# Softmax turned without normalising: inverted sums through DRAM scale the product with v, and both full tiles of even head pairs go by the crossbar (56 for 28)

## The chip, the cores and the metric

The kernel runs on one core of a Trainium2 chip. The metric is the device time of one execution in microseconds. Three executions of the kernel before took 923.4, 923.61 and 923.7 us; the median is 923.61. The engines are TensorE (PE, with its weight loads PEld), VectorE (DVE), ScalarE (ACT), GpSimd (POOL) and SyncE (SP), which here only issues DMAs.

## The reference

Attention over 8 batches of 8 heads (576 tokens, 64 features each). Scores more than tau below their row's maximum drop out before the softmax. A feed-forward part follows: a first product, relu, a convolution of three taps over the tokens, a gate, and a second product.

```python
scores = scale * np.matmul(q, k.transpose(0, 1, 3, 2))
thresh = np.max(scores, axis=-1, keepdims=True) - tau
scores = np.where(scores >= thresh, scores, -1000000000.0)
scores = scores - np.max(scores, axis=-1, keepdims=True)
attn = np.exp(scores)
attn = attn / (np.sum(attn, axis=-1, keepdims=True) + 1e-09)
attn_out = np.matmul(attn, v)
...
h = np.maximum(x @ w_in, 0.0)
conv_out += conv_w[k][None, None, :] * hp[:, k:k + S, :]
gate = 1.0 / (1.0 + np.exp(-conv_out))
return (h * gate @ w_out)
```

## The kernel before

The tokens of a batch are cut into tiles of 128 (four full ones and a last one of 64), and these into two chunks: tiles 0 and 1, and tiles 2, 3 and 4. The heads of a batch form four pairs; one pair of one chunk is a *pair* in what follows (64 in all, numbered 0 to 63), and one tile of one pair is a *unit* (160 in all). Odd pairs run their tiles backwards. Batch 0 ("plain") takes a path in full float32 and also prepares the weights; batches 1 to 7 split their operands into a high and a low part.

For each unit, `unit` (line 563) has TensorE compute the scores of both heads into PSUM (`ps_s`), VectorE take the negated maximum of a row (L599), ScalarE the exponential into `em` (L608), and VectorE the mask, which also adds up the rows into `few` (L611). Then come a guard against sums of zero (L628), the reciprocal (L635), an even share for a row whose sum is zero (L632), and the normalising of `em` in place, 128 x 576 for each head (L644, on POOL but for a few).

The normalised weights must be turned so that keys lie on partitions. `transposes` (L685) lets TensorE do it: for a full tile two groups of four 128 x 128 blocks and one block of a third group, which the tiles of a pair share (L703); ScalarE copies them out of PSUM (`ps_t`, two buffers) into `eT` (L698). For one full tile of each even pair of batches 1 to 7, 28 units in all, `cross` (L659) does it by DMA: ScalarE and POOL split `em` into low and high 16-bit halves (`parts`, L326 and L328), a DMA writes them to DRAM (`rows`, L676), and two DMA transposes read them back through the crossbar into `eT` (L681). `CROSS = (1, 0)` says how many full tiles of an even and an odd pair go that way.

`attend` (L746) multiplies `eT` with v into `pa`, which takes the same PSUM buffers as the transposes. From the third chunk on, two pairs are done together (28 joint products). ScalarE copies the result as the high part of `x` (L774), and VectorE subtracts for the low part (L777). `mm1` and `mm2` are the feed-forward products (`ph` and `po`), which run interleaved with the attention of the next chunk.

The order on each engine is fixed when the program is built: `Plan` simulates the engines with a planned duration for each step (the number after the engine's name in `op`), takes what is ready with the smallest rank minus `ahead`, and emits the instructions in that order. A step with `other` may go to another engine when its own has a backlog. DMAs are steps too (`put`, or `op("sp", ...)` with a `ring` cost). Each engine, SP included, works off its instructions in order and waits where its next one isn't ready. A buffer is free for its next use when its last reader is done; `eT`, `v`, `ps_t` have two each, `em` five.

## Time and profile before

| | before |
|---|---|
| median of three executions | 923.61 us |
| the profiled execution | 925.83 us, its span 924.0 us |
| mean granted TensorE clock | 0.989 |
| transposes on TensorE (L703) | 1060 |
| DMA transposes (L681) | 56 |
| normalising on POOL (L644) | 285, 258.5 us busy |

The page of a profile gives busy time, share of the span and number of instructions for each engine, then the chain of work that ended last, and the costliest groups of instructions: `line engine operation out<-in shapes xcount | busy us, mean ns of one | idle us of the engine just before them <- what ended most of it`. Rows of the view by windows give the length of a stretch, for each engine its busy us and (x number of instructions), then the granted clock, the share of the 16 DMA engines that is busy, and GB/s. Rows of waits read `engine line waited for: us in total, times, longest us`. A row of the chain or the timeline begins with its start and its length in us. TensorE's matmuls overlap one another, so the length of one is more than what it adds to the queue.

### The profile page before, as it was taken

To read this page: it belongs to the slowest core of one execution; us is meant where nothing else is said; L and a number is where in the kernel's file an instruction comes from. 1 tells how busy PE (TensorE), PEld (TensorE's weight loads), DVE (VectorE), ACT (ScalarE), POOL (GpSimd) and SP (SyncE) were. 2 spreads that over 40 slices of the span, in tenths; PEclk is the share of its full clock that TensorE was granted. 3 is DMA by queue.
4 is the path that set the end of the run, shared out by engine and by line. 5 is a ranking of instruction groups with operands and counts; after the bars stand their busy time and mean duration, and the time that the engine had idled before them with its cause. 6 is when DMAs were issued, how large, how long until landed. Compare 5 with 4: busy or idle time off the path is not lost.

```text
span 924.0 us, 18493 instructions
## 1 busy us (share of the span) xinstructions
PE 883.6 (96%) x6056; PEld 709.9 (77%) x6056; DVE 775.4 (84%) x1863; ACT 684.6 (74%) x1450; POOL 636.5 (69%) x1044
## 2 busy tenths in 40 slices
PE   5879899999999999999899999999999999999998
PEld 2445578768879788878778788887868878887897
DVE  5989999988998789987789779996979879998543
ACT  5868688778877787878668687877857778786643
POOL 3656867877777677876667778886866858785422
PEclk9989999999999999999899999999999999999999
DMA  5545137546563565526645275536647076543000
GB/s 207 168 152 158 44 113 210 120 132 181 141 172 76 153 178 158 148 73 175 166 123 126 86 183 138 158 92 181 169 114 180 29 194 169 131 120 100 14 23 35
DMA packets 120927, 122.28 MB, mean 132 GB/s; under 512 B 72320, under 2 KB 88960, under 8 KB 120832
## 3 DMA queue, kind: packets, MB, share of 16 engines
q1 hardware_dynamic: 119968, 119.20, 47.7%
q10 hardware_dynamic: 864, 1.90, 0.6%
q8 instruction: 49, 0.80, 0.4%
q14 instruction: 46, 0.38, 0.1%
HBM read 66.22 MB, written 25.95 MB: 100 GB/s over the span
## 4 chain that ended last, share of the span: by engine, by line
PE 63%; DVE 12%; ACT 10%; POOL 6%; DMA 5%; issue 4%; SPq 1%; ACTq 0%; DVEq 0%; POOLq 0%
PE po L853 17%; PE ph L795 13%; PE pa L767 10%; PE ps_s L591 9%; PE ps_t L703 9%; DVE em L611 4%; ACT em L608 3%; PE ps_s L584 3%; DVE few L599 3%; DMA xq<-in_qd_dram 2%; ACT eT L698 2%; POOL em L644 2%; PE pa L758 2%; DVE t L817 2%; DVE t L822 2%
## 5 line engine op out<-in xcount | busy, mean ns | idle before, releaser
L644 POOL TENSOR_SCALAR em<-em,few 128x576 f32<-128x576 f32 x285 | 258.5, 915 | 34.0 <-DVE few L635 22.4
L611 DVE SCALAR_TENSOR_TENSOR em<-ps_s,few,em 128x576 f32<-128x576 f32 x288 | 230.6, 812 | 38.2 <-ACT em L608 25.4
L608 ACT ACTIVATE em<-ps_s,few 128x576 f32<-128x576 f32 x288 | 210.4, 741 | 51.7 <-DVE few L599 43.1
L599 DVE TENSOR_REDUCE few<-ps_s 128x1 f32<-128x576 f32 x288 | 212.3, 749 | 35.5 <-PE ps_s L591 17.3
L795 PE MATMUL ph<-x,w1h 128*128 128x322 f32 (+1 forms) x1024 | 240.0, 306 | 0.9 <-ACT hp L810 0.6
L698 ACT ACTIVATE eT<-ps_t 128x512 f32<-128x512 f32 (+2 forms) x360 | 168.2, 487 | 31.2 <-PE ps_t L703 28.3
L795 PEld LDWEIGHTS ph<-x,w1h 128*128 128x128 f32 x1024 | 175.6, 191 | 6.3 <-issue 3.2
L703 PE MATMUL ps_t<-ident,em 128*128 128x128 f32 x1060 | 160.3, 280 | 9.6 <-POOL em L644 5.0
L591 PE MATMUL ps_s<-ks,q 128*128 128x288 f32 x896 | 158.9, 307 | 8.5 <-DVE em L611 5.9
L703 PEld LDWEIGHTS ps_t<-ident,em 128*128 128x128 f32 x1060 | 126.2, 143 | 34.4 <-POOL em L644 14.6
L795 PE MATMUL ph<-x,w1l 128*128 128x322 f32 (+1 forms) x512 | 151.9, 297 | 0.0
L591 PEld LDWEIGHTS ps_s<-ks,q 128*128 128x128 f32 x896 | 129.9, 190 | 26.7 <-issue 7.4
L333 POOL TENSOR_TENSOR gl<-t,gh 128x255 fp32r<-128x255 f32 (+9 forms) x192 | 122.7, 652 | 27.9 <-ACT gh L832 26.5
L767 PE MATMUL pa<-eT,v 128*64 128x320 f32 (+1 forms) x1024 | 132.1, 409 | 0.0
L853 PE MATMUL po<-w2h,gh 128*128 128x512 f32 x288 | 119.0, 413 | 0.4 <-ACT hp L810 0.4
L767 PEld LDWEIGHTS pa<-eT,v 128*64 128x64 f32 x1024 | 70.3, 137 | 59.4 <-issue 15.9
L853 PE MATMUL po<-w2h,gl 128*128 128x512 f32 x288 | 113.6, 395 | 0.2
L853 PE MATMUL po<-w2l,gh 128*128 128x512 f32 x288 | 113.5, 394 | 0.0
L817 DVE SCALAR_TENSOR_TENSOR t<-hp,cr 128x321 f32<-128x321 f32 (+1 forms) x128 | 85.1, 668 | 20.2 <-ACT hp L810 20.1
L795 PEld LDWEIGHTS ph<-x,w1l 128*128 128x128 f32 x512 | 97.7, 191 | 0.3
L817 DVE SCALAR_TENSOR_TENSOR t<-hp,cr,t 128x321 f32<-128x321 f32 (+1 forms) x128 | 91.9, 719 | 0.4
L824 ACT ACTIVATE t<-t,cm 128x321 f32<-128x321 f32 (+1 forms) x128 | 68.3, 534 | 28.3 <-DVE t L817 17.6
(81 smaller groups left out, 1147.9 us busy)
## 6 DMA issues: line engine op xcount, KB each, us to landing
v<-in_vc_dram SPq DMA_DIRECT2D x64, 288.0 KB, 3.9
rows<-parts SPq DMA_DIRECT2D x28, 576.0 KB, 3.2
k<-in_kp_dram SPq DMA_DIRECT2D x35, 320.0 KB, 3.5
out_dram<-ot SPq DMA_DIRECT2D x36, 256.0 KB, 2.1
xq<-in_qd_dram SPq DMA_DIRECT2D x28, 320.0 KB, 3.7
xk<-in_kt_dram SPq DMA_DIRECT2D x28, 288.0 KB, 3.3
ks<-xk SPq DMA_DIRECT2D x56, 144.0 KB, 3.6
xq<-in_qd_dram SPq DMA_DIRECT2D x28, 256.0 KB, 3.7
```

Source lines behind the costliest of these rows:

```text
L333: engines[e].tensor_tensor(dst, x, y, op=ALU.subtract)
L591: nc.tensor.matmul(ps[:, c, :CH], lhsT=q[:, h, o:o + n], rhs=k[:, h, c * CH:(c + 1) * CH], start=(i == 0), stop=(i == 1))
L599: nc.vector.tensor_reduce(few[:rows, nm], ps[:rows, :, :CH], op=ALU.max, axis=mybir.AxisListType.XY, negate=True)
L608: nc.scalar.activation(view(), ps[:rows, :, :CH], AF.Exp, bias=few[:rows, nm])
L611: nc.vector.scalar_tensor_tensor(view(), ps[:rows, :, :CH], few[:rows, th], view(), op0=ALU.is_ge, op1=ALU.mult, accum_out=few[:rows, total])
L644: engines[e].tensor_scalar(sl, sl, by, to, op0=ALU.mult, op1=ALU.add)
L698: "act", act(w, True), lambda dst=dst, src=src: nc.scalar.activation(dst(), src(pt), AF.Copy),
L703: nc.tensor.transpose(out=pt[:, at:at + P], in_=em[:, int(b * P):int(b * P) + P], identity=ident[:])
L767: nc.tensor.matmul(pa[j * D:(j + 1) * D, :w], lhsT=vt[:, blk, :], rhs=eT[:, :w // D, blk, :], start=False, stop=(r == 3))
L795: nc.tensor.matmul(ph[:, :an], lhsT=w1[w][:, cb, fs], rhs=xs[cb][:, h, :an], start=(cb == 0 and i == 0), stop=(cb == NCB - 1 and i == 2))
L817: nc.vector.scalar_tensor_tensor(t[:, :kn], hp[:, k:kn + k], cr[:, j, f:f + 1], y, op0=ALU.mult, op1=ALU.add)
L853: nc.tensor.matmul(po[:], lhsT=x[:, f, at:at + P], rhs=w[:, f, :], start=(f == 0 and i == 0), stop=(f == NFB - 1 and i == 2))
```

## The change

`em` is no longer normalised. The masked sums go into one tile `tot` per pair (a column for each tile and head), and when all units of the pair are masked, `invert` guards and inverts them, stores them as a row in DRAM (an element of four bytes per partition and tile, one or two DMAs per head) and loads that row back, spread over the 64 partitions of each head (`inv`). The product with v is then multiplied by `inv` on VectorE (`xn`), and the high and low part of `x` are taken from `xn`, the low part on POOL. A row whose sum is zero gets its even share from a tiny constant instead: ScalarE adds 2^-80 while it copies transposes out of PSUM, and the high halves of crossed tiles are raised to the bits of that value (a maximum on POOL). `CROSS = (2, 0)` sends both full tiles of an even pair by DMA, 56 units instead of 28. `em` has four buffers instead of five.

```diff
-NORM = (('pool',), ('pool',))
-NEAR = 8
+EVEN = 2.0 ** -80
+EVEN_TOP = 0x1780
+INVS = 2
+PARTS = 2
-EMS = 5
-CROSS = (1, 0)
+EMS = 4
+CROSS = (2, 0)
...
             def mask(ps=ps, th=th, view=view, total=total):
                 nc.vector.scalar_tensor_tensor(
                     view(), ps[:rows, :, :CH], few[:rows, th], view(), op0=ALU.is_ge, op1=ALU.mult,
-                    accum_out=few[:rows, total]
+                    accum_out=tot[:rows, total]
                 )
...
-        op("dve", 112, guard, w=[(few, "inverse")], r=ss, ahead=a, port=True, other=tiny)
-        op("dve", 82, lambda: nc.vector.reciprocal(few[:rows, inverse], few[:rows, inverse]), w=[(few, "inverse")], ahead=a)
-        op("dve", 124, even, w=[(few, "shift")], r=ss, ahead=a, port=True, other=tiny)
-        for h in range(m):
-            def norm(e, h=h):
...
+    def invert(i, p, n, tot):
+        cols, a = 2 * (n // P) + (n % P > 0), AHEAD["a"]
+        spread = plan.buf(wk, "inv", INVS, [P, S - QW], F32, f"inv_{i}")
+        row = plan.buf(far, "row", INVS, [2, S - QW], F32, f"row_{i}")
+        ts = [(tot, j) for j in range(cols)]
         def guard(e):
+            engines[e].tensor_scalar(tot[:, :cols], tot[:, :cols], S * EVEN, 1.0, op0=ALU.add, op1=ALU.mult)
+        op("dve", 112, guard, w=ts, ahead=a, port=True, other=[("pool", 200)])
+        op("dve", 82, lambda: nc.vector.reciprocal(tot[:, :cols], tot[:, :cols]), w=ts, ahead=a)
+        for h in range(2):
+            def out(h=h):
+                nc.sync.dma_start(
+                    row[h, :n // P * P].rearrange("(t q) -> q t", q=P), tot[:, :n // P * 2].rearrange("q (t h) -> q t h", h=2)[:, :, h]
+                )
+            op("sp", 500, out, w=[(row, h)], r=ts, ahead=a, ring=n // P * P * 1.6)
+            if n % P:
+                op(
+                    "sp", 500, lambda h=h: nc.sync.dma_start(row[h, n // P * P:n].rearrange("(q e) -> q e", e=1), tot[h * D:(h + 1) * D, cols - 1:cols]),
+                    w=[(row, 2 + h)], r=ts, ahead=a, ring=D * 1.6
+                )
+        for h in range(2):
+            j = h ^ p % 2
+            put(
+                n, lambda h=h, j=j: nc.sync.dma_start(spread[j * D:(j + 1) * D, :n], row[h:h + 1, :n].broadcast_to([D, n])),
+                issue=500, rows=D, w=[(spread, j)], r=[(row, h)] + ([(row, 2 + h)] if n % P else []), ahead=a
+            )
+        return spread
...
-                copy(e, parts[:, j], src)
+                if j:
+                    engines[e].tensor_scalar(parts[:, j], src, EVEN_TOP, None, op0=ALU.max)
+                else:
+                    copy(e, parts[:, j], src)
...
-                    "act", act(w, True), lambda dst=dst, src=src: nc.scalar.activation(dst(), src(pt), AF.Copy),
+                    "act", act(w, True), lambda dst=dst, src=src: nc.scalar.activation(dst(), src(pt), AF.Copy, bias=EVEN),
...
-            def high(pa=pa, x=x, off=off):
-                nc.scalar.activation(x[:, 0, off:off + w], pa[:, :w], AF.Copy)
-            def low(pa=pa, x=x, off=off):
-                nc.vector.tensor_tensor(x[:, 1, off:off + w], pa[:, :w], x[:, 0, off:off + w].bitcast(F32), op=ALU.subtract)
-            op("act", act(w, True), high, w=[(x, 0)], r=[(pa, 0)], ahead=a)
-            op("dve", dve(w), low, w=[(x, 1)], r=[(pa, 0), (x, 0)], ahead=a)
+            xn = plan.buf(wk, "xn", 2, [P, S - QW], F32, f"xn_{i}")
+            def scale(pa=pa, xn=xn, inv=inv):
+                nc.vector.tensor_tensor(xn[:, :w], pa[:, :w], inv[:, :w], op=ALU.mult)
+            def high(xn=xn, x=x, off=off):
+                nc.scalar.activation(x[:, 0, off:off + w], xn[:, :w], AF.Copy)
+            def low(e, xn=xn, x=x, off=off):
+                subtract(e, x[:, 1, off:off + w], xn[:, :w], x[:, 0, off:off + w].bitcast(F32))
+            op("dve", dve(w), scale, w=[(xn, 0)], r=[(pa, 0), (inv, 0), (inv, 1)], ahead=a)
+            op("act", act(w), high, w=[(x, 0)], r=[(xn, 0)], ahead=a)
+            op("pool", pool(w), low, w=[(x, 1)], r=[(xn, 0), (x, 0)], ahead=a, other=[("dve", dve(w))], port=True)
```

The change moves instructions everywhere, since every order is planned anew. Three places matter later. The first is TensorE after the scores of pair 9's first tile (`ps_s`), early in batch 1. Before, it turns the second full tile of pair 8 (`em_1398`) there; in between stands a group of `po` and the scores of the next tile:

```order
L703 MATMUL ps_t_0_1507<-ident,em_1398 128x128 x4
L703 MATMUL ps_t_4_1517<-ident,em_1398 128x128 x4
L853 MATMUL po_1325<-w2h,gh 128x512
L853 MATMUL po_1325<-w2h,gl 128x512
L853 MATMUL po_1325<-w2l,gh 128x512
L591 MATMUL ps_s_0_1534<-ks_1_1357,q_9_1372 128x288
L591 MATMUL ps_s_0_1534<-ks_1_1357,q_9_1448 128x288
L591 MATMUL ps_s_0_1534<-ks_1_1357,q_9_1372 128x288
L591 MATMUL ps_s_0_1534<-ks_1_1357,q_9_1448 128x288
L703 MATMUL ps_t_8_1541<-ident,em_1398 128x128
```

Of the change, the same place (after the product `pa_1464` of pair 7) up to the first transposes, which are of pair 9:

```order
L867 MATMUL po_1309<-w2h,gh 128x512
L867 MATMUL po_1309<-w2h,gl 128x512
L867 MATMUL po_1309<-w2l,gh 128x512
L593 MATMUL ps_s_0_1509<-ks_1_1363,q_9_1408 128x288
L593 MATMUL ps_s_0_1509<-ks_1_1363,q_9_1427 128x288
...
L593 MATMUL ps_s_1_1515<-ks_1_1363,q_9_1408 128x288
L593 MATMUL ps_s_1_1515<-ks_1_1363,q_9_1427 128x288
L711 MATMUL ps_t_0_1526<-ident,em_1481 128x128 x4
```

The nine transposes of pair 8's second tile are gone; what is left on TensorE is the same work in another order.

The second place is SP's queue around pair 20 (a second chunk of batch 2). Before, one half tile (`rows`) goes out, and its two turns stand between the loads of `v`:

```order
L676 DMA rows_3367<-parts_3336 128x2304
L551 DMA k_3372<-in_kp_dram 128x640
L541 DMA xq_3383<-in_qd_dram 128x2x320
L560 DMA v_3428<-in_vc_dram 128x576
L681 DMA_TRANSPOSE eT_3433<-rows_3367 128x9x128 x2
L560 DMA v_3481<-in_vc_dram 128x576
L551 DMA k_3492<-in_kp_dram 128x640
```

Of the change, from that load of `v` on, where `row` is the stored inverse and `inv` its spread:

```order
L561 DMA v_3464<-in_vc_dram 128x576
L689 DMA_TRANSPOSE eT_3473<-rows_3309 128x9x128 x2
L561 DMA v_3530<-in_vc_dram 128x576
L642 DMA row_3537<-tot_3235 128x2x1
L689 DMA_TRANSPOSE eT_3473<-rows_3369 128x9x128 x2
L649 DMA row_3537<-tot_3235 64x1
...
L649 DMA row_3682<-tot_3387 64x1
L684 DMA rows_3721<-parts_3695 128x2304
L655 DMA inv_3729<-row_3537 64x320 x2
L875 DMA out_dram<-ot_3707 128x512
L655 DMA inv_3748<-row_3682 64x320 x2
L684 DMA rows_3770<-parts_3761 128x2304
```

The same stretch of the queue has four turns instead of two, eight stores of inverses and four spreads; half tiles, outputs and the loads of the next pairs stand behind spreads that wait for their stores.

The third place is VectorE, from the reciprocal of pair 21 (`tot_3387`) to the scaling of the joint product of pairs 20 and 21 (`xn_3827`, `xn_3848`). Before, two subtractions that read only the product and its high part stood there:

```order
L635 RECIPROCAL few_3857<-few_3857 128x1
L777 TENSOR_TENSOR x_3676<-pa_3849,x_3676 128x320
L777 TENSOR_TENSOR x_3683<-pa_3852,x_3683 128x320
L599 TENSOR_REDUCE few_3927<-ps_s_0_3910 128x1
L599 TENSOR_REDUCE few_3927<-ps_s_1_3921 128x1
```

Of the change (left out are three more maxima, three limits and three masks):

```order
L639 RECIPROCAL tot_3387<-tot_3387 128x5
L613 SCALAR_TENSOR_TENSOR em_3643,tot_3665<-ps_s_1_3616,few_3636,em_3643 128x576
L601 TENSOR_REDUCE few_3698<-ps_s_0_3684 128x1
...
L613 SCALAR_TENSOR_TENSOR em_3807,tot_3817<-ps_s_0_3782,few_3798,em_3807 128x576
L639 RECIPROCAL tot_3665<-tot_3665 128x5
L784 TENSOR_TENSOR xn_3827<-pa_3790,inv_3729 128x320
L784 TENSOR_TENSOR xn_3848<-pa_3793,inv_3748 128x320
L601 TENSOR_REDUCE few_3860<-ps_s_0_3841 128x1
L601 TENSOR_REDUCE few_3860<-ps_s_1_3854 128x1
```

The scaling stands where the subtraction stood, but reads `inv` too, which comes by two DMAs after the reciprocal at the head of these rows; the maxima of the next scores stand behind it.

40 lines of the change are left out of this document (13 added, 27 removed).

## The prediction

> **What bounds the kernel now.** The views, in order: the page's busy table, the busy times by stretch, TensorE's waits from 120 to 880 us.
>
> ```profile
> span 924.0 us, 18493 instructions
> PE 883.6 (96%) x6056; PEld 709.9 (77%) x6056; DVE 775.4 (84%) x1863; ACT 684.6 (74%) x1450; POOL 636.5 (69%) x1044
> ```
> ```profile
> core 0: us, PE busy (x) PEld busy (x) DVE busy (x) ACT busy (x) POOL busy (x), PEclk, DMA share, GB/s
> 120.00:860.00 740.00, 726.83 (x5128) 601.26 (x5125) 646.98 (x1565) 569.63 (x1207) 549.29 (x897) 0.99 0.53 140
> 0.00:120.00 120.00, 96.33 (x561) 56.17 (x561) 102.04 (x250) 86.07 (x173) 69.38 (x110) 0.96 0.44 141
> 860.00:924.00 64.00, 60.48 (x373) 52.46 (x371) 26.34 (x50) 28.93 (x72) 17.82 (x39) 1.00 0.07 25
> ```
> The average hides three stages. From 120 to 860 us TensorE is idle for only 740.0 - 726.8 = 13.2 us, while VectorE has 93 us to spare: there TensorE's own work sets the pace, and its largest wait there is small:
>
> ```profile
> PE ps_s L591 <- DVE em L611: 5.9, 8, 2.1
> ```
> In the first 120 us TensorE idles 23.7 us and VectorE is the fullest engine (102 of 120, and it also prepares the weights). After 860 us TensorE works off the last products. So work taken off TensorE shortens the middle one for one; work taken off VectorE counts in the first stage; work taken off POOL counts by itself nowhere.
>
> **What leaves TensorE.** In each of 28 even pairs of batches 1 to 7 the second full tile is turned by DMA too. That removes two groups of four transposes and one of the odd ones, nine a tile: 28 x 9 = 252 of 1060 at the line that turns. Their price is read from the chain of waits in a stretch where TensorE never stops, since a matmul's own length overlaps the next one's:
>
> ```profile
> 408.15 0.33 PE ps_t L703 x3
> ...
> 419.70 0.87 PE ps_t L703 x8
> ```
> 0.33/3 and 0.87/8 both give 0.109 to 0.110 us, so 252 x 0.109 = **27.5 us**. No other matmul is added or removed. All of it lies in the stage where TensorE is the bound.
>
> **What leaves the other engines**, by the page's and the grouped rows:
>
> ```profile
> L644 POOL TENSOR_SCALAR em<-em,few 128x576 f32<-128x576 f32 x285 | 258.5, 915 | 34.0 <-DVE few L635 22.4
> ```
> ```profile
> L635 DVE RECIPROCAL few<-few 128x2 f32<-128x2 f32 x128 | 20.3, 159 | 0.7
> L628 DVE TENSOR_SCALAR few<-few 128x2 f32<-128x2 f32 x56 | 20.3, 362 | 1.0
> ```
> The normalising goes (258.5 us of POOL), and the guard, the reciprocal and the even share are no longer done per tile (160 times): one guard and one reciprocal per pair remain (64 each). In the first stage, where VectorE counts, the guard (L628), the even share (L632) and the reciprocal (L635) take on VectorE, in that order:
>
> ```profile
> 0.00:120.00 120.00, 2.02 (x6) 4.05 (x13) 0.96 0.44 141
> 0.00:120.00 120.00, 3.81 (x17) 0.45 (x2) 0.96 0.44 141
> 0.00:120.00 120.00, 2.94 (x19) 0.96 0.44 141
> ```
> 2.02 + 3.81 + 2.94 = 8.8 us. Eight pairs' reciprocals (8 x 0.159) and, of their guards, the share that stays on VectorE (27 of 64 in the new order, so 3.4 x 0.362) put back 2.5. Of the 6.3 us I count the share that VectorE is busy there (85%): **5.3 us**. Bounds: 0, if PE's idle time there comes from loads, and the 23.7 us of that idle time.
>
> **What is added on engines**, by groups of like form:
>
> ```profile
> L698 ACT ACTIVATE eT<-ps_t 128x512 f32<-128x512 f32 x232 | 135.2, 598 | 29.6 <-PE ps_t L703 27.8 <-DMA rows<-parts 0.5
> L326 ACT ACTIVATE parts<-em 128x1152 uint16<-128x1152 uint16 x28 | 32.6, 1166 | 1.8 <-POOL em L644 1.6
> L328 POOL COPY parts<-em 128x1152 uint16<-128x1152 uint16 x27 | 32.8, 1216 | 0.6
> L380 POOL TENSOR_SCALAR stage_f<-stage_f 128x512 f32<-128x512 f32 x16 | 10.3, 648 | 8.3 <-ACT stage_f L377 7.9
> L333 POOL TENSOR_TENSOR gl<-t,gh 128x320 fp32r<-128x320 f32 x8 | 6.9, 868 | 0.3 <-ACT gh L832 0.3
> L777 DVE TENSOR_TENSOR x<-pa,x 128x320 fp32r<-128x320 f32 x32 | 15.6, 486 | 17.0 <-ACT x L774 16.9
> ```
> ACT: 28 more halves (28 x 1.166 = 32.6 us) against 56 evictions of 512 fewer (56 x 0.598 = 33.5): nothing. VectorE: the scaling by the inverse reads PSUM and SBUF as the old subtraction did, 64 at its price, so they cancel. POOL takes that subtraction (64 x at most 0.868 = 56 us) and 56 high halves, now with a maximum. This form is not in the trace: per element between the copy (1216/1152 = 1.06 ns) and the normalising (915/576 = 1.59), so 1.22 to 1.83 us; by the two-limit row (648/512 = 1.27 ns) I take 1.46, 82 us. POOL gains 56 + 82 - 33 = 105 and loses 258: it gets emptier and hides both. Without that cover they would still not count, as TensorE is the bound.
>
> **What is added on DMA and its queue.** 28 more half tiles go out, 56 more turns come in, and new are 192 tiny stores (one element of four bytes per partition and tile) and 128 spreads over 64 partitions. First the page's row of the queue, then SP's timeline, then the windows around it:
>
> ```profile
> q1 hardware_dynamic: 119968, 119.20, 47.7%
> ```
> ```profile
> 475.06 3.18 SPq L681 DMA_TRANSPOSE eT<-rows  x2
> ```
> ```profile
> 476.00:482.00 6.00, 6.00 (x39) 5.22 (x36) 3.79 (x9) 4.12 (x8) 3.21 (x5) 1.00 0.96 228
> ```
> In these 6 us two turns, a load of v and one output keep the engines 0.96 busy. If all of it were the turns', one would cost all 16 engines 2.9 us; with the two plain transfers (288 and 256 KB on the page) taken out by bytes against the 228 GB/s of the row, 1.7. I take 2: 56 x 2 = 112 us, and 114 for half tiles and spreads (an estimate: 28 x 576 KB and 128 x some 72 KB at the same rate). What the tiny stores cost is bounded by the small packets of the turns:
>
> ```profile
> DMA packets 3048, 2.27 MB, mean 189 GB/s; under 512 B 2441, under 2 KB 2441, under 8 KB 3047
> ```
> The row is DMA's for 470 to 482 us: two turns are the only small packets there, 2441 in about 4 us, or 1.6 ns each. The stores write 32 x 2 x (256 + 320) = 36,864 elements: 59 us. So DMA goes from 0.48 x 924 = 444 us to about 729, or 0.81 of the new span: not the bound, but crowded. SP itself issues the 56 turns in 1.6 us each (3.18/2) and some 350 short ones in 0.5 us each (the median of the row below), 265 us more; it has room, since it waits 210 us for outputs alone:
>
> ```profile
> L510 SPq DMA_DIRECT2D ks<-xk x56: 461/538/1156, 94.6 to 777.3; - x56
> ```
> ```profile
> SPq L861 <- ACT ot L860: 210.2, 27, 24.3
> ```
> But the spreads wait on SP for their stores, and behind them stand the loads of the next pairs, the half tiles and the outputs. The Trainium skill, "DMA: Bandwidth & Descriptors", § Rules for kernel authors, speaks against these stores: a last dimension that isn't contiguous becomes one descriptor per element. No row here shows such a store; by the 10.5 ns a packet that the page's § Bandwidth gives for 64 packets, as an estimate, they would take 387 us and fill the engines beyond the span, and the crowding case below would be the likeliest, 909 us.
>
> What does crowding cost TensorE? The trace has two cases (ScalarE's waits of 2.72 and 3.11 us for xq at L553), in which a load came late beside two turns; ACT waited for it, VectorE for ACT, TensorE for VectorE. This is the dearer one, in the timeline and in the windows:
>
> ```profile
> 448.83 0.31 ACT L553 ACTIVATE q<-xq 128x128 f32<-128x128 f32 x1 [2.72 <-DMA xq<-in_qd_dram]
> ...
> 450.75 1.04 PE L591 MATMUL ps_s<-ks,q 128*128 128x288 f32 x4 [1.87 <-DVE em L611]
> ...
> 673.81 0.31 ACT L553 ACTIVATE q<-xq 128x128 f32<-128x128 f32 x1 [3.11 <-DMA xq<-in_qd_dram]
> ```
> ```profile
> 448.00:458.00 10.00, 7.54 (x38) 6.98 (x37) 7.05 (x17) 5.70 (x14) 6.90 (x10) 0.66 0.62 147
> ```
> In these 10 us TensorE idles 10 - 7.5 = 2.5 us, and the granted clock is 0.66 on average, which costs 0.34 x 10 = 3.4 us: 5.9 us for one such stall. I take **one more of them, 5.9 us**; bounds are none, and one at the start of each of seven batches, 41 us. The Trainium skill, "TensorE: Matmul & The Clock Gate", § Part 1: The HAM clock gate, lets the clock halve only after an idle window of about 3.4 us. By that rule a stall of 2.5 us costs no clock, and the sum would be 3.4 us less; the trace disagrees, its clock fell after gaps shorter than that.
>
> The turned tiles themselves should arrive in time (timeline of SP and of TensorE, and the turns' landing):
>
> ```profile
> 416.31 3.51 SPq L681 DMA_TRANSPOSE eT<-rows  x2
> ```
> ```profile
> 438.55 0.77 PE L758 MATMUL pa<-eT,v 64*64 64x320 f32 x8
> ```
> ```profile
> DMA to landing us min/median/max: 3.7/4.6/6.4
> ```
> Four turns instead of two issue in 7 us from 416.3 and land by 428 to 430, some 9 us ahead of the product at 438.55 that reads them.
>
> **The sum**, on the profiled span: 924.0 - 27.5 - 5.3 + 5.9 = 897.1. That execution took 925.8 with what lies around its span, 2.2 over the median of 923.61; I carry the difference of -26.9 over to the median: **896.7 us**.
>
> **The rivals.**
> - *Crowded DMA* (more late loads like the one above): three stalls instead of one give 924.0 - 32.8 + 17.7 - 0.4 = 909 us. For it speaks the share of 0.96 over six us, to which two more turns come; against it, only two such stalls beside 28 crossed tiles now.
> - *The scaling waits for its inverse; this ends slower.* Stores and loads of ks stand in for the two hops (first the output's row, then the one of ks):
>
> ```profile
> DMA to landing us min/median/max: 2.0/2.1/5.0
> ```
> ```profile
> DMA to landing us min/median/max: 2.2/3.5/5.6
> ```
> After the odd pair's reciprocal SP issues four stores (0.5 us each), waits for them, spreads twice (1.0) and lands: 2 + 2.1 + 1 + 3.5 = 8.6 us at the medians, 13.6 at the worst. Between that reciprocal and the scaling VectorE has, in the order shown for the change, five masks, four maxima and the even pair's scaling:
>
> ```profile
> L611 DVE SCALAR_TENSOR_TENSOR em<-ps_s,few,em 128x576 f32<-128x576 f32 x288 | 230.6, 812 | 38.2 <-ACT em L608 25.4
> L599 DVE TENSOR_REDUCE few<-ps_s 128x1 f32<-128x576 f32 x288 | 212.3, 749 | 35.5 <-PE ps_s L591 17.3
> ```
> 5 x 0.812 + 4 x 0.749 + 0.486 = 7.5 us, 8.6 at 87% busy. So the inverse is just in time at the medians and 5 us late at the worst. Behind a waiting scaling stand VectorE's next maxima, and both PSUM buffers of the transposes stay taken, so TensorE runs dry soon after. At the midpoint, 2.5 us late at each of 28 joint products, 70 us: 924.0 - 32.8 + 70 - 0.4 = 961. It turns slower from 32.8/28 = 1.2 us a product. Against it: the worst landings are rare, the even pair's inverse has a whole pair more, and TensorE has FFN products that need neither buffer.
> - *Better than forecast*: an emptier POOL and a shorter way from mask to transposes remove TensorE's 13.2 us too, and no stall is added: 924.0 - 32.8 - 10 - 0.4 = 881.
> - *It doesn't pay*: TensorE's time comes off, but ACT or DMA paces the middle at today's rate: 918 to 923.
>
> **How the numbers follow.** Forecast (884 to 905) 0.70, crowded 0.13, inverse late 0.07, better 0.08, no gain 0.02. The range takes the forecast's own and half of the crowded case, and its upper end some of the inverse's: 884 to 914 us. A measurement tells 0.2% (1.8 us) from no change. Faster: 0.70 + 0.08 + 0.12 = 0.90; within 0.2%: 0.03; slower: 0.07.
>
> **What would show it.** In the new profile: 808 transposes at about 0.109 us in the chain, TensorE busy near 856 us and still above 93% of the span; POOL near 480; no wait of the scaling for a DMA beyond a few us in all; the granted clock at 0.5 in no more than one or two stretches after 120 us; TensorE's idle time in the first 120 us down by some 5 us. Waits of VectorE's scaling for the inverse, of TensorE's products for the turned tiles, or of SP's loads behind the spreads would make the forecast wrong.

## The result, and the profile after

| | before | after |
|---|---|---|
| median of the runs | 923.65 us (4 runs) | 1347.86 us (4 runs) |
| ratio | | 1.458, 95% interval 1.447 to 1.470 |
| profiled span | 924.0 us | 1349.3 us |
| mean granted TensorE clock | 0.989 | 0.858 |

The forecast was 896.7 us, in a range of 884 to 914; the change makes the kernel 46% slower. The page of the changed kernel first: its span, its busy table and its DMA queue (packets, MB, share of 16 engines).

```profile
span 1349.3 us, 18039 instructions
PE 968.8 (72%) x5804; PEld 753.4 (56%) x5804; DVE 767.6 (57%) x1594; ACT 684.6 (51%) x1376; POOL 551.6 (41%) x783
q1 hardware_dynamic: 240480, 161.84, 70.9%
```

No engine is full any more: TensorE had 96% of its span, now 72%. So it waits, and the views of waits say for what. SP's queue, then the engines:

```profile
SPq L655 <- DMA row<-tot: 279.1, 64, 9.4
SPq L875 <- ACT ot L874: 50.3, 7, 20.7
SPq L689 <- DMA rows<-parts: 28.4, 12, 7.0
```
```profile
DVE xn L784 <- DMA inv<-row: 211.1, 34, 16.7
ACT q L543 <- DMA xq<-in_qd_dram: 122.3, 21, 13.1
PE ps_s L593 <- DVE em L613: 83.2, 26, 13.3
```

SP stands 279 us at the spreads until the stores of inverses have landed, 4.4 us each time; before, its largest wait was for outputs. What stands behind it comes late: the inverses themselves (211 us of VectorE's scaling) and the loads of the next queries (122 us of ScalarE). One such place in SP's timeline (start, length, instruction):

```profile
581.83 3.08 SPq L689 DMA_TRANSPOSE eT<-rows  x2
...
590.21 0.49 SPq L649 DMA_DIRECT2D row<-tot  x1
590.79 6.91 SPq L689 DMA_TRANSPOSE eT<-rows  x2
...
601.46 1.37 SPq L642 DMA_DIRECT2D row<-tot  x1
602.87 0.48 SPq L649 DMA_DIRECT2D row<-tot  x1
612.03 0.36 SPq L684 DMA_DIRECT2D rows<-parts  x1
```

A pair of turns that doesn't follow a store takes 3.08 us to issue; the pair right behind one takes 6.91. Then, after the last store, nothing is issued for 9 us. The chain of waits (start, length, what) names what TensorE's next product stands for, and SP's next half tile (612.03) goes out 0.07 us after the same landing; the windows show the engines meanwhile:

```profile
592.48 19.48 DMA eT<-rows
611.96 0.14 issue
612.10 1.35 PE pa L766 x8
```
```profile
core 0: us, PE busy (x) PEld busy (x) DVE busy (x) ACT busy (x) POOL busy (x), PEclk, DMA share, GB/s
600.00:602.00 2.00, 2.00 (x13) 1.82 (x12) 0.89 (x3) 1.93 (x6) 1.91 (x2) 1.00 1.02 154
602.00:604.00 2.00, 2.00 (x10) 1.60 (x10) 1.10 (x3) 2.00 (x4) 1.88 (x2) 1.00 0.23 42
606.00:608.00 2.00, 0.55 (x12) 0.04 (x4) 1.64 (x3) 2.00 (x4) 2.00 (x1) 1.00 0.00 0
610.00:612.00 2.00, 0.00 (x0) 0.00 (x0) 0.00 (x0) 0.00 (x0) 0.20 (x1) 0.75 0.00 0
```

The turn behind the stores lands after 19.5 us, where the forecast's row of before had 6.4 at most. By the records no transfer starts at 606 to 608 and at 610 to 612 us (the view counts a transfer where it starts), and yet it has not landed; TensorE runs dry, and its clock falls to 0.75. A second, separate surprise is in the page's groups:

```profile
L673 POOL TENSOR_SCALAR parts<-em 128x1152 uint16<-128x1152 uint16 x56 | 177.9, 3176 | 43.9 <-DVE em L613 34.5
```

The maximum on 16-bit halves takes 3.18 us. The copy that it replaces took 1.22, and the forecast had put it at 1.46.

### The profile page after: what moved, and what is told of

The parts are those of the page before. It is cut to its first block, busy times and chain, and to the rows that moved or that the text cites. A ratio compares the mean times of both kernels' runs of the same rounds, so it can differ in the third digit from the quotient of the medians.

```text
span 1349.3 us, 18039 instructions
## 1 busy us (share of the span) xinstructions
PE 968.8 (72%) x5804; PEld 753.4 (56%) x5804; DVE 767.6 (57%) x1594; ACT 684.6 (51%) x1376; POOL 551.6 (41%) x783
## 4 chain that ended last, share of the span: by engine, by line
DMA 32%; PE 12%; SPq 12%; DVE 5%; issue 3%; ACT 3%; POOL 3%; DVEq 0%; POOLq 0%; ACTq 0%
DMA row<-tot 16%; SPq L689 8%; DMA xq<-in_qd_dram 5%; PE ph L809 4%; PE po L867 3%; DMA rows<-parts 3%; PE ps_s L593 2%; DMA inv<-row 2%; DMA ks<-xk 2%; DMA xk<-in_kt_dram 2%; DMA eT<-rows 1%; PE pa L775 1%; DVE few L601 1%; POOL parts L673 1%; DVE t L831 1%
## 5 line engine op out<-in xcount | busy, mean ns | idle before, releaser
L593 PE MATMUL ps_s<-ks,q 128*128 128x288 f32 x896 | 181.5, 337 | 154.1 <-DVE em L613 83.2
L711 PE MATMUL ps_t<-ident,em 128*128 128x128 f32 x808 | 132.7, 297 | 91.5 <-DVE xn L784 79.6
L673 POOL TENSOR_SCALAR parts<-em 128x1152 uint16<-128x1152 uint16 x56 | 177.9, 3176 | 43.9 <-DVE em L613 34.5
L784 DVE TENSOR_TENSOR xn<-pa,inv 128x256 f32<-128x256 f32 (+1 forms) x64 | 29.2, 456 | 263.9 <-DMA inv<-row 211.1
L711 PEld LDWEIGHTS ps_t<-ident,em 128*128 128x128 f32 x808 | 104.7, 152 | 112.3 <-DVE xn L784 79.4
L706 ACT ACTIVATE eT<-ps_t 128x512 f32<-128x512 f32 (+2 forms) x276 | 128.4, 482 | 28.6 <-PE ps_t L711 26.6
L334 POOL TENSOR_TENSOR gl<-t,gh 128x255 fp32r<-128x255 f32 (+14 forms) x191 | 116.3, 622 | 54.1 <-ACT gh L846 49.1
L334 POOL TENSOR_TENSOR x<-xn,x 128x256 fp32r<-128x256 f32 (+1 forms) x64 | 48.6, 762 | 194.3 <-ACT x L787 191.3
L334 POOL TENSOR_TENSOR q<-xq,q 128x512 fp32r<-128x512 f32 x56 | 72.9, 1302 | 123.4 <-ACT q L543 123.1
L607 POOL TENSOR_SCALAR few<-few,ntau 128x1 f32<-128x1 f32 x162 | 55.0, 340 | 154.9 <-DVE few L601 137.1
```

The lines of the kernel that those rows point to most:

```text
L334: engines[e].tensor_tensor(dst, x, y, op=ALU.subtract)
L593: nc.tensor.matmul(ps[:, c, :CH], lhsT=q[:, h, o:o + n], rhs=k[:, h, c * CH:(c + 1) * CH], start=(i == 0), stop=(i == 1))
L673: engines[e].tensor_scalar(parts[:, j], src, EVEN_TOP, None, op0=ALU.max)
L706: "act", act(w, True), lambda dst=dst, src=src: nc.scalar.activation(dst(), src(pt), AF.Copy, bias=EVEN),
L711: nc.tensor.transpose(out=pt[:, at:at + P], in_=em[:, int(b * P):int(b * P) + P], identity=ident[:])
```

## The experiments

Three theories stood at the start: the four-byte stores land late and hold up what follows (A); 28 more crossed tiles overload DMA (B); the trip through DRAM costs whatever the stores look like (C). Each run was timed beside the kernel before; ratios are to that.

### Crossing alone, and the trip alone

The kernel before with one edit, `CROSS = (2, 0)`, everything else as it was; and the changed kernel with the edit undone.

```diff
-CROSS = (1, 0)
+CROSS = (2, 0)
```

> The kernel before with both full tiles of even pairs crossed (56 for 28) and nothing else. Theory A, the stores of single elements are what costs (they land late, SP waits for them, and they slow the turns queued behind them): 890 to 905 us, the 27.5 us of TensorE's transposes come off. Theory B, 28 more crossed tiles overload the DMA engines: over 1150 us. Theory C, the trip through DRAM costs whatever the shape of its stores (store, wait on SP, spread): as A, 890 to 905.

> The changed kernel with one crossed tile per even pair as before (28), so the unnormalised turn and the trip of the inverse alone. Theory A: 1150 to 1300 us. Theory B: 920 to 1000 us. Theory C: 1150 to 1300.

Crossing alone: 922.8 us, ratio 0.999 (0.995 to 1.003). The trip alone: 1216.1 us, 1.317 (1.307 to 1.328). So B falls: by themselves, twice as many crossed tiles don't make the kernel slower. Beside the four-byte stores they do cost 1347.9 - 1216.1 = 132 us, 28 more maxima among it. But alone they gain nothing either, where theory A expected 890 to 905 us, and that speaks against my forecast. The window of the middle stage and a wait of TensorE, crossing alone:

```profile
120.00:860.00 740.00, 707.64 (x4898) 575.20 (x4899) 653.60 (x1584) 573.58 (x1175) 569.84 (x887) 1.00 0.70 185
```
```profile
PE ps_s L591 <- DVE em L611: 14.1, 17, 1.8
```

Of the same stretch TensorE was busy 726.83 us before. 19 us of its work went, and it idles 32.4 us instead of 13.2. Over the whole span its busy time fell by 883.6 - 861.8 = 21.8 us, where the forecast had taken off 27.5.

### Wide stores, and stores on another queue

Two kernels with every step of the change in its order. In one, each store writes pieces of 512 bytes from a constant tile; in the other the four-byte stores are issued by ScalarE instead of SP. Shown are the stores of full tiles; those of the last tiles are changed likewise.

```diff
-                    row[h, :n // P * P].rearrange("(t q) -> q t", q=P), tot[:, :n // P * 2].rearrange("q (t h) -> q t h", h=2)[:, :, h]
+                    row[h, :n // P * P].rearrange("(t q) -> t q", q=P), ident[:n // P, :]
```
```diff
-                nc.sync.dma_start(
+                nc.scalar.dma_start(
...
-            op("sp", 500, out, w=[(row, h)], r=ts, ahead=a, ring=n // P * P * 1.6)
+            op("act", 500, out, w=[(row, h)], r=ts, ahead=a, ring=n // P * P * 1.6)
```

> The changed kernel in its own order on every engine, but each store of a row of the inverse writes 512 bytes per descriptor from the identity tile instead of 4 bytes from the sums; the spreads then bring zeros and ones, so the normalising is left out of the result. Number of DMAs, the waits of the spreads on SP and the crossed tiles stay. Theory A: 890 to 940 us, and SP's waits for the stores under 100 us. Theory B: above 1300 us. Theory C: above 1200 us, SP's waits near 280 us.

> The changed kernel with the stores of the inverse issued by ScalarE's DMA queue instead of SP's; the spreads and all else stay on SP. Theory A, where the single elements hold only what stands behind them in their own queue: the turns go back from 3 us and more to about 1.6 us each on SP, and the time falls to 1000 to 1250 us. Theory A, where they hold the DMA engines that both queues share: 1300 us or more and the turns stay slow. Theory B: about 1350 us.

Wide stores: 972.6 us, 1.054 (1.049 to 1.058). On ScalarE's queue: 1428.4 us, 1.547 (1.537 to 1.558). The shape of the stores alone is 1347.9 - 972.6 = 375 us, nearly all of the loss. A stands, though 972.6 lies above its 890 to 940, so something else costs too; of C at most 49 us are left. SP's waits for the stores at the spreads fall from 279.1 us to 13.8 (15 of them), the scaling hardly waits, and the queue's share of engines falls:

```profile
DVE xn L782 <- DMA inv<-row: 14.3, 6, 5.5
```
```profile
q1 hardware_dynamic: 201184, 161.83, 62.3%
```

0.709 x 1349.3 - 0.623 x 968.9 = 353 us of all 16 engines went with the shape of 36,864 elements. They are not the elements' own time. Where ScalarE issues the stores, its queue (q10) carries them apart from SP's (q1); before, q10 had 864 packets and 0.6%:

```profile
q1 hardware_dynamic: 200544, 161.68, 72.3%
q10 hardware_dynamic: 40800, 2.06, 2.9%
```

The queue with the stores took 0.029 x 1422.4 = 41 us, while SP's queue, without one of them, took 0.723 x 1422.4 = 1028 us, where it had 604 with wide stores. The packet records of the changed kernel's own trace say the same. Its 51,680 packets of four bytes took 34 us of the 16 engines; with wide stores 12,064 of that size remain, with 7 us. So the stores themselves took 27 us, less than the 59 that I had put down at 1.6 ns, the price of the turns' packets. The other 326 us are other transfers whose packets last long: 2143 packets of SP's queue took over 1 us, 317 us in all, and only 21 of them had four bytes; with wide stores there were 181, with 15 us. The stores hold up what the engines do for others, whichever queue they come from.

### Who waits: unread stores, wider pieces, elements apart

Three variants of the changed kernel ask what makes a four-byte store dear. In the first the spreads read an input, so that nobody waits for a store. In the second a partition's two numbers go as one piece of 8 bytes. The third is the first with 256 bytes between elements.

```diff
-    spread[j * D:(j + 1) * D, :n], row[h:h + 1, :n].broadcast_to([D, n])
+    spread[j * D:(j + 1) * D, :n], vc[0, 0, h:h + 1].rearrange("q k d -> q (k d)")[:, :n].broadcast_to([D, n])
```
```diff
-    row[h, :n // P * P].rearrange("(t q) -> q t", q=P), tot[:, :n // P * 2].rearrange("q (t h) -> q t h", h=2)[:, :, h]
+    row[h, :n // P * P].rearrange("(q t) -> q t", q=P), tot[:, h * (n // P):(h + 1) * (n // P)]
```
```diff
-        row = plan.buf(far, "row", INVS, [2, S - QW], F32, f"row_{i}")
+        row = plan.buf(far, "row", INVS, [2, S - QW, D], F32, f"row_{i}")
...
-    row[h, :n // P * P].rearrange("(t q) -> q t", q=P)
+    row[h, :n // P * P, 0].rearrange("(t q) -> q t", q=P)
```

> The changed kernel with its four-byte stores as they are, but the two spreads of a pair read an input in DRAM (the start of v) instead of the row just stored: nobody waits for a store to land. The normalising is so left out of the result (it is scaled by other numbers); all instructions and their order stay. Theory A1 (SP stands at the spreads until the stores land, 279 us in the changed kernel's waits, and that is the cost): the wait is gone and the time falls to the 972 us of the wide stores, 965 to 1000. Theory A2 (the small stores hold up every DMA behind them, whoever reads them): the wait moves to the next DMAs (turns of 4 to 5 us, loads), and the time stays above 1200 us. In between, the time says how the 375 us divide.

> The changed kernel with each store of two full tiles written as 128 descriptors of 8 bytes (a partition's two numbers side by side) instead of 256 of 4 bytes; the 64 elements of a last tile stay as they are. The inverted sums so come back in another order, and the result is scaled by the wrong rows' sums. A store of two full tiles is then half as many descriptors with the same bytes. If the cost goes by the number of descriptors, the stores of the first chunk fall from 256 to 128 and those of the second from 320 to 192, and the changed kernel's 375 us of them fall by 45%, to a time near 1180 us. If it goes by the DMA (one landing for each store, however small its pieces), the time stays near 1348 us.

> The run with unread stores (1259 us), with each four-byte element stored 256 bytes from the next instead of side by side in DRAM: as many descriptors, as many bytes, in the same order. As there, the normalising is left out of the result. If neighbouring elements cost because several DMA engines write into the same short stretch of DRAM at once, the cost goes and the time falls towards 972 us; if each descriptor costs by itself, it stays near 1259 us.

Unread: 1259.2 us, 1.367 (1.355 to 1.380). Pieces of 8 bytes: 1098.6 us, 1.193 (1.189 to 1.196). Elements apart, and unread: 981.5 us, 1.063 (1.057 to 1.069). So the waits at the spreads are only 89 of the 375 us; 287 stay when nobody reads the stores. And of these, 278 go when the same number of descriptors, with the same bytes in the same order, write 256 bytes apart. The turns' issue (min, median, max in ns) of the unread run and of the one apart, and the latter's queue and landing of stores:

```profile
L689 SPq DMA_TRANSPOSE eT<-rows x112: 1272/1722/10028, 161.6 to 1191.8; - x112
```
```profile
L689 SPq DMA_TRANSPOSE eT<-rows x112: 1278/1566/2849, 140.4 to 919.0; - x112
q1 hardware_dynamic: 240480, 161.84, 64.1%
DMA to landing us min/median/max: 1.5/2.6/5.9
```

It is not the descriptor that costs: apart, the 36,864 take 0.641 x 983.6 - 603.6 = 27 us of the engines, 0.7 ns each, as much as side by side; but only 247 packets last over 1 us, 22 us in all. It is that neighbours of four bytes are written into one short stretch of DRAM. That they come through several DMA engines at once and wait for one another there is my reading; only the distance was varied. The run with 8-byte pieces, two neighbours in one descriptor, fits: 44% fewer descriptors took away 66% of the loss (249 of 375 us), more than a cost per descriptor would.

### The maximum on GpSimd

The kernel with wide stores, with a plain copy for the maximum; and the same kernel (with its maximum) with one crossed tile.

```diff
-                    engines[e].tensor_scalar(parts[:, j], src, EVEN_TOP, None, op0=ALU.max)
+                    copy(e, parts[:, j], src)
```
```diff
-CROSS = (2, 0)
+CROSS = (1, 0)
```

> The kernel with wide stores (972 us) with GpSimd's high half as a plain copy instead of the maximum, 56 times, in the same order; the normalising and the even share of crossed rows are left out of the result. GpSimd's copy of this shape took 1.22 us before, the maximum 3.18. Theory D1 (what is left above 923 us is the long maximum: GpSimd stands in it while the thresholds of the next scores wait behind it): 56 x 1.96 us = 110 us of GpSimd go, of which those on the way to the mask come off, and the time falls to 925 to 940 us. Theory D2 (what is left is SP's further DMAs and the wait of the scaling): the time stays at 965 to 972 us.

> The kernel with wide stores (972 us) with one full tile of an even pair turned by DMA instead of two (28 units, as before the change), all orders planned anew; the normalising is left out of the result. 28 of the 56 maxima on GpSimd go, and 252 transposes come back to TensorE. Theory D1 (the maximum is what is left): the time falls by about half of the 49 us, to 940 to 950 us, since TensorE's transposes cost nothing in the run that changed them alone (0.9991). Theory D2 (the trip and the scaling, the same for all 64 pairs): it stays at 965 to 975 us. If TensorE's 27 us were worth their time here, it would rise to 990.

With a copy: 908.6 us, 0.987 (0.984 to 0.989). With one tile, so 28 maxima: 943.6 us, 1.025 (1.019 to 1.030). The maximum accounts for 972.6 - 908.6 = 64 us, more than the 32 to 48 I expected and more than the 49 that the wide stores had left. The run with half of the maxima is 29 us faster, about half of that, if its 28 fewer crossings are worth nothing there, which no run separates. The busy tables, with the maximum and with a copy:

```profile
PE 871.5 (90%) x5804; PEld 688.5 (71%) x5804; DVE 776.5 (80%) x1594; ACT 681.2 (70%) x1376; POOL 557.8 (58%) x783
```
```profile
PE 857.4 (95%) x5804; PEld 685.7 (76%) x5804; DVE 724.8 (80%) x1594; ACT 677.5 (75%) x1376; POOL 452.4 (50%) x783
```

GpSimd's 105 us less were to be seen coming. But VectorE, with the same 1594 instructions, is 52 us less busy too: its operations between SBUF tiles (`t` of the feed-forward, the guard of `tot`) last longer beside the maximum, the masks, which read PSUM, do not. With the maximum, then with a copy:

```profile
L613 DVE SCALAR_TENSOR_TENSOR em<-ps_s,few,em 128x576 f32<-128x576 f32 x288 | 229.7, 811 | 39.2 <-ACT em L610 20.9 <-POOL few L607 14.6 <-ACT few L605 0.6
L829 DVE SCALAR_TENSOR_TENSOR t<-hp,cr 128x321 f32<-128x321 f32 x64 | 52.7, 830 | 15.5 <-ACT hp L822 14.3 <-POOL gl L334 1.2
L636 DVE TENSOR_SCALAR tot<-tot 128x4 f32<-128x4 f32 x16 | 25.5, 1594 | 0.2
```
```profile
L613 DVE SCALAR_TENSOR_TENSOR em<-ps_s,few,em 128x576 f32<-128x576 f32 x288 | 230.0, 812 | 21.4 <-ACT em L610 17.4 <-ACT gh L844 0.6 <-POOL hp L817 0.3
L829 DVE SCALAR_TENSOR_TENSOR t<-hp,cr 128x321 f32<-128x321 f32 x64 | 43.6, 688 | 15.5 <-ACT hp L822 14.3 <-POOL gl L334 1.2
L636 DVE TENSOR_SCALAR tot<-tot 128x4 f32<-128x4 f32 x16 | 8.2, 513 | 0.2
```

A guard of 128 x 4 numbers takes 1.6 us instead of 0.5: it seems to stand behind the maximum on something that both engines need, though no run shows which part of the chip that is. Besides, masks wait for thresholds that GpSimd computes behind the maximum, 14.6 us in the mask's first row, and not among the largest in its second. So TensorE's scores wait for the masks. With the maximum, then with a copy:

```profile
PE ps_s L593 <- DVE em L613: 27.9, 29, 3.2
```
```profile
PE ps_s L593 <- DVE em L613: 4.1, 7, 1.2
```

The pair of runs shows that the maximum costs the 64 us; the way they take over VectorE and the masks is read from these rows.

### What hides the transposes' time

With wide stores and a copy the time is 1.3% under the kernel before. Is that TensorE's 27.5 us? Two pairs of runs, each with one and with two crossed tiles: the kernel before without normalising, and the kernel before with a row maximum over 64 of 576 scores.

```diff
-        for h in range(m):
+        for h in range(0):
             def norm(e, h=h):
```
```diff
-    nc.vector.tensor_reduce(few[:rows, nm], ps[:rows, :, :CH], op=ALU.max, axis=mybir.AxisListType.XY, negate=True)
+    nc.vector.tensor_reduce(few[:rows, nm], ps[:rows, :, :32], op=ALU.max, axis=mybir.AxisListType.XY, negate=True)
```

> The kernel before without the normalising (288 operations, nearly all on GpSimd, left out: the result is not normalised); sums, guards, reciprocals and shares stay; one full tile of even pairs by DMA as before. It is the base of the next run. What it gains itself: if normalising on GpSimd, off the busy TensorE, were hidden, 0; by the waits of TensorE for it (its transposes wait 5.0 us for it in all) at most some 5 to 15 us: 910 to 923.

> The run before it, also without the normalising, with both full tiles of even pairs by DMA: the 252 transposes go. With normalising in place this edit gained nothing (0.9991); in the runs with turned sums it was worth 30 us. If normalising on GpSimd was what hid the gain (it stands between the mask and the transposes, and now between the mask and the halves that GpSimd copies), the gain is here 20 to 30 us. If VectorE's chain from score to mask hid it, it is here under 8 us as well, and the 30 us have another cause.

> The kernel before with the row maximum on VectorE taken over 64 of 576 scores (288 reductions that took 749 ns each; so thresholds and weights are others than the reference's). It takes about 288 x 0.6 = 170 us off VectorE's 775 us and shortens the chain from score to mask by 0.6 us. Theory (VectorE's chain sets the pace beside TensorE): with VectorE relieved, TensorE fills its gaps, of the 40 us that it idles in all some 10 to 25 us go, and the time is 900 to 915 us. Rival (VectorE has no part in the pace): 918 to 924 us.

> The same with both full tiles of even pairs by DMA, that is the run that changed the crossing alone (0.9991), with VectorE relieved. Theory (the score chain over VectorE is what hid the 27 us of transposes): they now come out, and it is 20 to 27 us faster than the run with a short maximum and one tile. Rival (the gain is lost elsewhere, in GpSimd's or ScalarE's further work on the crossed halves or in the time to the end of the turns): it is under 8 us faster.

Without normalising: 907.1 us with one tile (0.984, 0.981 to 0.987), 909.9 with two (0.987, 0.982 to 0.991). With a short maximum: 913.6 (0.989, 0.987 to 0.991) and 909.8 (0.986, 0.984 to 0.988). The middle stage without normalising, one tile and then two:

```profile
120.00:860.00 740.00, 729.96 (x5247) 610.42 (x5247) 634.75 (x1543) 569.95 (x1220) 348.38 (x697) 1.00 0.51 139
```
```profile
120.00:860.00 740.00, 716.92 (x5018) 589.92 (x5017) 660.71 (x1579) 572.12 (x1170) 375.46 (x703) 0.99 0.70 184
```

Two things follow. Leaving the normalising out gains 15 us by itself, though it ran on an engine that was 69% busy and my forecast gave it nothing: that is about what the run with a copy gains (908.6). The short maximum gains 9 us by itself. And crossing 28 more tiles changes the time by +2.8 and -3.8 us here: what TensorE is spared, it idles. Neither normalising nor VectorE's maxima hide it; both expectations of a gain of 20 us or more failed. What does hide it is open. One row points somewhere: scores that wait for masks, without normalising with one tile and then two.

```profile
PE ps_s L591 <- DVE em L611: 2.5, 5, 1.1
```
```profile
PE ps_s L591 <- DVE em L611: 10.4, 11, 2.4
```

It grew from 5.9 to 14.1 us with crossing alone and from 2.6 to 8.6 with the short maximum: 6 to 8 us each time, of the 13 to 19 that TensorE idles more in the middle stage. Every order here was planned anew, and no run takes transposes away with the order held, so the order itself is an untested rival for a part.

### Looking for a version that keeps the gain

Five kernels do the whole computation with stores of 128 bytes or more and without the maximum. An empty row can only come from a negative tau, so the threshold is then set to keep all keys, and the scores are scaled to zero. The first takes one TensorE transpose of a pair's sums and the reciprocal behind it; the second has one tile by DMA instead of two; the third takes the reciprocal first and scales q or k instead of the exponent; the fourth and fifth turn on VectorE, with two tiles and with one. Of each, only the statements that do it are shown, without the steps around them; the third `diff` belongs to the third kernel, the last to the fourth and fifth.

```diff
+        pt = plan.buf(ps_t, "ps_t", 2, [P, 512], F32, f"it_{i}")
+        nc.tensor.transpose(out=pt[:cols, :P], in_=tot[:, :cols], identity=ident[:])
...
+        nc.vector.reciprocal(spread[:cols, :P], pt[:cols, :P])
...
+        nc.sync.dma_start(row[h, :m * P].rearrange("(t q) -> t q", q=P), spread[h * m:(h + 1) * m, :P])
```
```diff
-CROSS = (2, 0)
+CROSS = (1, 0)
```
```diff
+        nc.vector.reciprocal(tot[:, :cols], tot[:, :cols])
...
         nc.tensor.transpose(out=pt[:cols, :P], in_=tot[:, :cols], identity=ident[:])
-        nc.vector.reciprocal(spread[:cols, :P], pt[:cols, :P])
+        copy(e, spread[:cols, :P], pt[:cols, :P])
```
```diff
+        nc.vector.reciprocal(flat[:, :cols], tot[:, :cols])
+        nc.vector.transpose(spread[:, :32], flat[:])
...
+        nc.sync.dma_start(row[h, t * P:(t + 1) * P].rearrange("(b q) -> b q", q=32), spread[c:P:32, :32])
```

> The whole computation, with the parts of the change that paid kept and the two that cost it replaced. The masked sums of a pair (128 partitions x 4 or 5 columns, now ordered by head) are turned by one TensorE transpose into 4 or 5 rows of 128, VectorE takes their reciprocals out of PSUM, and the stores write 512 bytes a descriptor, as in the wide runs; then the same spreads and scaling. The maximum on GpSimd, the constant added in the copies from PSUM and the guard go: a row without a survivor only comes with a negative tau, and for that case the threshold is set so low that all keys stay and the exponential's scale is set to zero, both from the sign of tau, once. Theory (small stores and long maximum are all that was wrong): the time is that of the wide stores with a copy, 908.6 us, plus 64 further transposes on TensorE and their hold of the PSUM buffers that transposes and the product with v share: 908 to 916 us, under the 921 to 924 of before. Rival (the further use of those two buffers stalls TensorE by a microsecond for each of 64 pairs): 925 to 970 us.

> The run with turned sums, but one full tile of an even pair by DMA instead of two (28 units, as before the change); orders planned anew. It prices the 28 further crossings once the normalising is gone from GpSimd. If TensorE's saved transposes count one for one, as my forecast had it, it is 27 us slower than the run with two tiles; if they are hidden as in the run that changed them alone on the kernel before (0.9991), it is within 5 us of it.

> The run with turned sums (927.7 us) with its two dear operations replaced; the whole computation. The reciprocals are taken before the turn, on 128 partitions x 4 or 5 columns (0.17 to 0.18 us in the wide run, against 0.94 us for 4 or 5 partitions x 128), and a copy on ScalarE brings the turned row out of PSUM; and the sign of tau scales q or k where they are prepared (72 operations) instead of the 288 exponentials (829 ns with a scale per partition, 740 without). That takes 64 x 0.77 = 49 us off VectorE and about 25 us off ScalarE's exponentials, on which the masks wait. Theory (these two are the 19 us above the wide run with a copy): 905 to 916 us, faster than before. Rival (the turn through the PSUM buffers that transposes and products share costs the 19 us): 920 to 928 us.

> The run with turned inverses (927.6 us) with the turn on VectorE: it transposes the inverted sums in 32 x 32 blocks, and one store for each tile and head writes four pieces of 128 bytes side by side into the row (four to six stores for a pair instead of two to four). The 64 turns go off TensorE, whose busy time there was 874.0 us against 857.4 in the wide run with a copy, and off the PSUM buffers. The whole computation. Theory (the turn on TensorE is the 19 us): 64 transposes of some 0.2 us on VectorE and 128 further issues of 0.25 us on SP lie beside the rest, and the time is 905 to 916 us, faster than before. Rival (pieces of 128 bytes side by side still hold each other up, or SP's further stores delay the spreads): 918 to 950 us.

> The run with the turn on VectorE, with one full tile of even pairs by DMA instead of two; the whole computation, orders planned anew. If the 30 us between the two runs with turned sums came from TensorE's transposes, it is 20 to 30 us slower than the run with two tiles; if they came from the PSUM buffers that transposes, products and turned sums shared there, it is within 6 us of it, as on the kernel before.

| | two tiles | one tile |
|---|---|---|
| turned sums | 927.7 us, 1.005 (1.003 to 1.007) | 957.5 us, 1.036 (1.032 to 1.040) |
| turned inverses | 927.6 us, 1.006 (1.003 to 1.009) | |
| turn on VectorE | 939.1 us, 1.016 (1.013 to 1.018) | 946.5 us, 1.025 (1.023 to 1.027) |

None beats the kernel before, and the first lies 19 us above the run with wide stores and a copy (908.6). In it, two operations were dearer than I had thought (the exponential with a scale per partition; the reciprocal of 128 numbers on each of a few partitions):

```profile
L611 ACT ACTIVATE em<-ps_s,few,some 128x576 f32<-128x576 f32 x288 | 232.9, 829 | 49.6 <-DVE few L602 47.0
L641 DVE RECIPROCAL inv<-it 5x128 f32<-5x128 f32 x32 | 30.1, 940 | 3.2 <-PE it L638 3.0
```

Replacing both moved the time by nothing, so they were not the 19 us; my theory fell there. What the third still has over the run with a copy is above all the turn itself on TensorE, whose busy time is 874.0 us against 857.4:

```profile
L639 PE MATMUL it<-ident,tot 128*5 128x128 f32 x32 | 8.8, 275 | 2.3 <-ACT eT L708 2.3
L639 PE MATMUL it<-ident,tot 128*4 128x128 f32 x32 | 8.7, 272 | 0.9 <-ACT eT L708 0.5 <-DVE tot L636 0.2
```

With the turn on VectorE, TensorE's busy time is back at 863.8 us, but it idles 937.3 - 863.8 = 73.5 us where the run with a copy has 49.0. SP issues 320 stores at half a microsecond, where the wide run issued 192 at 0.25 to 0.28, and SP and DMA are 19% of the chain that ended last, where they are 7% with turned inverses. The two chains, inverses turned on TensorE and on VectorE, and the latter's SP:

```profile
PE 63%; DVE 11%; ACT 10%; DMA 6%; issue 6%; POOL 2%; SPq 1%; ACTq 0%; DVEq 0%; POOLq 0%
```
```profile
PE 52%; DMA 12%; DVE 11%; ACT 9%; SPq 7%; issue 6%; POOL 2%; DVEq 0%; ACTq 0%; POOLq 0%
```
```profile
L645 SPq DMA_DIRECT2D row<-inv x256: 476/508/1279, 29.0 to 878.8; - x128
L655 SPq DMA_DIRECT2D inv<-row x128: 444/582/1513, 33.3 to 881.5; - x128
```

So turning the sums costs more than leaving the normalising out gains: the two runs lie 19 and 31 us above the run with a copy, against a gain of 15. That it is the turn is argued from these rows; the runs differ in other operations too.

The two tiles are worth 30 us with turned sums and 7 with the turn on VectorE, between the 20 to 30 and the 6 that I had set as signs. With turned sums the 30 us are TensorE's own work. One tile and then two:

```profile
PE 899.2 (94%) x6120; PEld 716.4 (75%) x6120; DVE 762.2 (80%) x1539; ACT 702.1 (73%) x1446; POOL 430.1 (45%) x734
```
```profile
PE 869.8 (94%) x5868; PEld 684.4 (74%) x5868; DVE 761.7 (82%) x1580; ACT 705.0 (76%) x1379; POOL 447.2 (48%) x732
```

Its busy time differs by 29.4 us, and its idle time (spans of 956.4 and 925.7 us) hardly, 57.2 and 55.9. Its waits for its PSUM buffers, which the turned sums need too, are 12.8 us with one tile and 2.1 with two, but other idle time makes up for that. So here transposes count one for one, as on the kernel before they do not; why, no run shows.

## Why the prediction was wrong

- **The tiny stores: the step that failed.** The forecast counted their own time alone: 59 us of DMA engines at 1.6 ns an element, in a total that was "not the bound, but crowded", and one late load of 5.9 us for the crowding. It let them land like an output's row (2.1 us). Their own time was no more than that, 27 us. What it put at nothing is what they do to the other transfers: these took 326 us more of the engines, SP stood 4.4 us at the spreads each time, and turns behind the stores took up to 10 us to issue. Together that was 375 us of time. The rule of the Trainium skill that I weighed ("DMA: Bandwidth & Descriptors", § Rules for kernel authors: a non-contiguous last dimension becomes one descriptor per element) pointed the right way, and the trace agrees with it: 40,800 packets on the queue that carried the stores. But a cost per descriptor is not what the runs show, since 256 bytes apart as many took 27 us and held up little. That the prediction's estimate of 387 us from it is near the 353 measured is luck, as nearly all of these are the time of other transfers; and even with it the prediction would have gone to 909 us.
- **The late inverse** had its mechanism right: "The scaling waits for its inverse", with TensorE dry behind it. It had 0.07 and 961 us, since I used the landing of ordinary rows; with wide stores the scaling waits 14.3 us in all, so at those landings it indeed does not decide. Nor is it the larger part: with unread stores only 89 of the 375 us go.
- **The maximum** at 1.46 us, with an upper bound of 1.83, was 3.18; it was also to be hidden, since GpSimd "gets emptier". It cost 64 us, by the traces by way of VectorE: 52 us of longer operations there, and masks that wait for thresholds. Whether an engine has time says nothing of what its work does to the others.
- **"work taken off TensorE shortens the middle one for one"**: 27.5 us were forecast; crossing alone took 21.8 off TensorE's busy time and gave 0.999 (0.995 to 1.003). Of the pairs of runs without the four-byte stores and the maximum, it held only in the one with turned sums. 13.2 us of idle time in 740 are no proof that nothing else is just as near.
- **"work taken off POOL counts by itself nowhere"**: normalising, left out alone, gave 0.984. In the run with wide stores and a copy, a gain came after all, but the forecast had it in the wrong place.
- **The first stage**: TensorE's busy time there went from 96.3 us to 97.2 in the run with a copy, so about 1 us of the 5.3.
- **Crowded DMA**, as far as it comes from the crossed tiles, was no cause by itself: crossing alone takes the middle stage's share from 0.53 to 0.70 and leaves the time as it was. Whether it ate part of what TensorE was spared there, no run separates; with turned sums a share of 0.74 went with the full gain.

Taken together: 908.6 us with wide stores and a copy, 64 for the maximum, 375 for the stores.

## What to carry to other kernels

Before a few hundred bytes go through DRAM, look at how they lie there: a column of single elements stored side by side, 147 KB in all, took 27 us of the DMA engines itself and made the transfers of 160 MB beside it, 604 us with wide stores, 326 us longer. Its cost falls on the others. An operation whose form the trace doesn't have should carry a range that reaches well above its nearest rows, and whether it is hidden should be asked of the instructions queued behind it and of the engines beside it, not of the share of its own. And where the busiest engine is at 96%, take some of its work away in a run by itself before counting that work as time.

## What the runs showed of the hardware

- Four-byte stores in DRAM took 0.7 ns each of all 16 DMA engines, side by side and 256 bytes apart alike. But side by side they held up other transfers: 2143 packets of over 1 us, against 247 apart and 181 with 512-byte pieces; and from another queue they did so too. A DMA transpose behind them landed after 19.5 us, the last part of it with no record of a transfer that starts.
- A maximum on 128 x 1152 16-bit numbers took GpSimd 3.18 us, a copy of them 1.23, and VectorE's operations between SBUF tiles took up to three times as long beside it (1594 ns against 513).
- An exponential of 128 x 576 took 829 ns with a scale per partition and 740 without; a reciprocal of 5 x 128 took 940 ns, of 128 x 5 183.
- One transpose of 128 x 5 on TensorE was 0.27 us of its busy time; within a group of transposes one had been 0.11.
